# A retention-then-MLP kernel on one core: attention of the third group of units joins the stretches, with new values for load order and layouts

## The chip, the core and the metric

The kernel runs on one core of a Trainium2 chip. Times are device microseconds of one execution, from start to end on that core. The time before is a median of three runs. Engines are named as in the profile: PE is TensorE (matmuls), PEld its weight loads, DVE is VectorE, ACT is ScalarE, POOL is GpSimd (here it issues the loads), SP is SyncE (stores, and transposing transfers).

## What is computed

A retention layer (attention with a decay in place of the softmax) and, on its output, an MLP with an exact GELU:

```python
B, H, S, D = 8, 8, 576, 64                       # q, k, v
scores = matmul(q, k^T) / sqrt(D)
gamma  = 1 - 2 ** (-5 - h)                       # one for each head
Dmat   = where(i >= j, gamma ** (i - j), 0)
ret    = matmul(scores * Dmat, v)                # [B, H, S, D]
x      = ret -> [B * S, H * D]                   # 4608 tokens x 512
h      = x @ w_in                                # 512 -> 2048
g      = 0.5 * h * (1 + erf(h / sqrt(2)))
out    = g @ w_out                               # 2048 -> 512
```

Inputs and output are float32; the products run in bfloat16, with sums in float32.

## The kernel before

**Units and groups.** A sequence of 576 rows is cut into five chunks of 128 rows, the last with 64. A unit is one chunk of one batch entry, for all eight heads; the two short last chunks of two batch entries share one unit. There are 36 units, and they are put in groups of two (the short one is a group of its own): group 0 is units 0 and 1, group 1 units 2 and 3, group 2, the third, units 4 and 5, and so on. Four units make one block of 512 tokens, the `xT` tile; there are nine blocks. Units 4 to 7 make the second block.

**Attention of a unit.** Q and K are transposed (units 0 to 9 on TensorE, `turn`, which writes `qk_ps`; later ones by a transposing transfer from SP). Then come `scores` (`sc`), a multiplication with the decay mask on VectorE (`ret`), the products with V inside the chunk (`inner`, into `o_ps`), the running sum of K times V over the chunks (`state`, into `u_ps`, copied to `u_sb`), and the products of Q with that sum (`cross`, into `o_ps` too). V is scaled by the decay first (`scaled_v`, L826 on VectorE as one product for all heads, L829 on ScalarE as eight activations of 64 columns); the list `VH_ACT` says which units' V goes to ScalarE. The result is copied into `xT` on the way out of the accumulators.

**MLP of a block.** The first GEMM gives `hT` or, from the third block on, in parts, the accumulators `yT`, `zT` and `xT_` of seven products in place of eight (Strassen's scheme on 2 x 2 parts: "units" of the layout, with sums of weights `wi_sum` and of tokens `xs`). `LAYOUTS` says for blocks 2 to 8 in which order the four quarters of the first GEMM run: '0' is quarter 0 by seven products, '01' two quarters interleaved, 'p3' quarter 3 plain, '3p2' a quarter by seven interleaved with a plain one. The second GEMM (`oT`) is plain in the first block and by seven products in the others (`w_sum`, `s`). In the first block the first GEMM can start on a part of the tokens: a pair of column blocks runs as four pieces of 128 tokens each (`CUTS`), as units become ready, unless it stands in the list `WIDE`; then it runs at the full 512 tokens, when all four units are there.

**What sets the order.** The order of all engines is fixed when the program is built. A planner (`Plan`) keeps a clock for each engine, gives every operation a duration, a due time and the operations that it needs, and at each step issues what can start first. MLP products come from `stream`; `LOOK` says how far ahead in it the planner may pick. From a certain group on, the attention on TensorE is not planned product by product but as a list (`macro_of`): `inner` of both units of the group, the states behind it, scores of the next group where it is not in `APART`, and `cross`, issued one behind the other by `run_all`, due at the group's need plus `SHIFT`. In this document such a list is a stretch. Scores of a group in `APART` are a list of their own, due `BEFORE` ahead. `EARLY` says for which groups the lists are made: with 3, from the fourth group on; the operations of the first three are planned one by one.

```python
for n in range(EARLY + 1, len(groups) + 1):
    macros += [(n, names, need[n - 1] + SHIFT[n]) for names in macro_of(n)]
    if n in APART:
        macros.append((n, scores_of(groups[n]), need[n] - BEFORE))
```

**Loads.** All but the first unit's Q, K and V come through one queue that POOL issues, in the order of `ORDER`: `k2` is K of unit 2, `wi0` one eighth of `w_in`, `wo0` of `w_out`, `pos` a small table made on POOL in between. Units from 11 on follow in order of number. At most eight transfers are in flight. A unit's Q, K or V arrives as 128 KB, a weight piece as 256 KB.

**Filler.** While the planner's TensorE clock is under 16 us, `warm` fills each planned gap with products of zeros, of 512 columns, or 128 for the rest of a gap; eight of 512 stand at the very start.

All matmuls are issued by the helper `product` (L231) and the transposes by `turned` (L235), so the profile's rows are told apart by tiles.

Of the kernel before, what the change touches and what calls it, by code (L numbers as in the profile page):

```python
# [107 lines left out]
def kernel(  # L108
# [52 lines left out]
    def slot_of(i):  # L161
# [9 lines left out]
    N_VH = 5  # L171
    N_RET = 3
    N_Q = 4
    VH_ACT = [5, 6, 7, 8, 9, 10, 21, 22, 23, 24, 26, 27, 28, 29, 30, 31, 33, 34, 35]
    HOT = 10.1
    N_WARM = 8
    SLACK = 0.2
    CUTS = (0, 128, 256, 384, 512)
    AHEAD = 6
    WIDE = [2, 10, 14, 12, 4]  # L180
    VH_DUE = 14.0
    PARTS = 4
    FAST = 1
# [1 line left out]
    BUSY_FETCH = 6.2  # L185
    GAP_A = 4.7
    GAP_B = 0
    SHIFT = {4: -0.5, 5: 4.0, 6: 4.5, 7: -2.0, 8: 6.0, 9: 0.5, 10: 0.5, 11: -6.0, 12: -3.5, 13: -0.5, 14: -3.5, 15: -0.5, 16: -4.5, 17: -2.0, 18: -3.5, 19: 0.0, 20: 1.0}
    APART = [3, 5, 6, 7]
    BEFORE = 8.1  # L190
    UNIT_FROM = 2
    LOOK = 12
    HOLD = 6
    LAYOUTS = {2: ['01', '2', 'p3'], 3: ['01', '2', 'p3'], 4: ['1', '02', 'p3'], 5: ['0', '1', '2', 'p3'], 6: ['01', '23'], 7: ['01', '23'], 8: ['0', '12', 'p3']}
    LEAD = 8.9
    SPREAD = 5.6
    EASE = 9
    ORDER = ("k2 k1 pos q1 wi0 q3 k3 q2 v1 v2 v3 wi4 wi7 wi1 wi5 v4 k4 q5 wi6 k5 wi3 wi2 q4 wo0 v5 wo4 wo1 q9 wo5 "
             "q8 v7 wo6 v6 q7 q6 wo2 k7 v10 wo7 wo3 k6 q10 k8 v8 k10 k9 v9").split()
    K_ORDER = [0, 1, 8, 9, 2, 3, 10, 11, 4, 5, 12, 13, 6, 7, 14, 15]  # L200
    PRODUCTS = "3251467"
    SECOND = "1267534"
# [1 line left out]
    for t in range(UNIT_FROM, N_BLK):  # L204
        LAYOUT[t] = LAYOUTS[t]

# [99 lines left out]
    for t in range(N_BLK):  # L306
        if t < 2:
            cuts = CUTS if t == 0 else (0, 256, 512)
            for lo, hi in zip(cuts, cuts[1:]):
                stream.append([("1", t, m, 2, lo, hi) for m in K_ORDER[::2] if t or m not in WIDE])  # L310
            if t == 0:
                stream.append([("1", t, m + n, 1, 0, TOK) for m in WIDE for n in range(2)])
        else:
# [44 lines left out]
    pos = const.tile([128, 1, NCI], FP32, name="pos")  # L358
# [121 lines left out]
    def tiles_of(i):  # L480

        if i not in loaded:
            n = slot_of(i)
            if i in kept:
                loaded[i] = (const.tile([128, 2, H, D], BF16, name=f"qk_ld{i}"), const.tile([128, H, D], BF16, name=f"v_ld{i}"))
                return loaded[i]
            if n not in slots:
                ld_ring.take()
                slots[n] = (ld_pool.tile([128, 2, H, 2, D], BF16, tag="qk", name="qk_ld"),
                            ld_pool.tile([128, 2, H, D], BF16, tag="v", name="v_ld"))  # L490
            qk, v_ld = slots[n]
            j = units[i][2] or 0
            if i in old:
                loaded[i] = (qk.rearrange("p a (j h) b d -> p j a (h b) d", j=2)[:, j], v_ld[:, j])
            else:
                loaded[i] = (qk[:, :, :, j], v_ld[:, j])
        return loaded[i]
# [42 lines left out]
    for i in range(11, N_U):  # L540
        ORDER += [f"{what}{i}" for what in "qkv"]
    prev = ["val"]
    for item in ORDER:
        what = item.rstrip("0123456789")
# [325 lines left out]
    for n in reversed(range(len(groups) - 1)):  # L870
        need[n] = min(need[n], need[n + 1] - SPREAD)
    tiles_of(0)
# [2 lines left out]
            lambda engine, nm=nm: copy_on(engine, loaded[0][1] if nm == "v" else loaded[0][0][:, "qk".index(nm)], first[nm]),  # L875
            7.0 if nm == "v" else 5.2, at=lambda nm=nm: cast_at[nm])
    land = {}
    EARLY = 3
    ALONE = [groups[n][0] for n in range(2, len(groups)) if n in APART or groups[n - 1][0] not in fine]
    for i in range(N_U):  # L880
        bp, ci, j = units[i]
# [51 lines left out]
    for i in v_order:  # L933
# [3 lines left out]
        before = ["dv", f"land v{i}"] + ([f"vh{v_order[n - 1]}"] if n else [])  # L937
        if i in VH_ACT:
            step_ = H // PARTS
# [472 lines left out]
    def macro_of(n):  # L1412


        back, front = groups[n - 1], groups[n] if n < len(groups) and n not in APART else []
        states = states_behind(n - 1)
        if back[0] in fine:
            a = [f"in_a{back[0]}"] + [f"st_a{bp},{ci}" for bp, ci in states]
            b = [f"in_b{back[0]}"] + [f"st_b{bp},{ci}" for bp, ci in states]
            if front:  # L1420
                a, b = a + [f"odd_{front[0]}"], b + [f"even_{front[0]}"]
            return [a, b]
        ahead = scores_of(front)
        olds = [f"state{bp},{ci}" for bp, ci in states]
        if back[0] in tails:
            return [olds + [f"in_t{back[0]}"] + ahead]
        return [[f"inner{i}" for i in back] + olds + ahead + [f"cross{i}" for i in back if units[i][1]]]

    def scores_of(front):
        return [f"both_{i}" if i in fine or i in tails else f"scores{i}" for i in front if i not in fine or i == slot_of(i)]  # L1430

    def states_behind(n):

        if n < 0:
            return []
        i = groups[n][0]
        bp, ci, j = units[i]
        if j is None:
            return [(1, 0)] if bp == 0 else []
        return [] if (bp, ci) == (1, 0) else [(bp, ci)]  # L1440

    assigned = {}
    macros = []
# [4 lines that stand above are left out]
    in_macro = {nm for m in macros for nm in m[1]}  # L1448
# [98 lines left out]
    def pe_candidates():  # L1547
# [11 lines left out]
        for run in heads:  # L1559
# [4 lines left out]
            else:  # L1564
                look = run[:LOOK]
            for one in look:
# [23 lines left out]
    while True:  # L1590
        got = []
        for e in ("act", "dve", "pool", "sp"):
            b_ = P.best(e, SLACK if T[e] < 20.0 and e != "pool" else 0.05)
            if b_:
# [8 lines left out]
        if e == "pe":  # L1603
# [9 lines left out]
            else:  # L1613
                for run in heads:
                    got = [one for one in run[:LOOK] if f"mlp{one}" == op.name]
                    if got:
# [46 lines left out]
```

## Time and profile before

| | us |
|---|---|
| median of 3 runs | 280.59 (280.51 to 280.66) |
| the profiled execution | 281.12 |
| its span, first to last instruction | 279.2 |
| PE busy | 273.0 |
| DVE busy | 228.7 |
| ACT busy | 181.7 |
| POOL busy | 110.4 |
| last matmul starts | 275.7 |

The profiled execution's time holds 1.9 us around the span. A matmul's busy time in the rows is longer than the time to the next one's start, since they overlap; where the row says that 8 matmuls took so long, the next row's start tells how far apart they were issued. Rows of the timeline have start, duration, engine, line, operation and tiles, the number merged, and in brackets the idle time before and what ended it ("issue" where nothing that the profile shows ended it).

### The profile page before, as it was taken

Reading aid. Unit: us, or ns where it says so; the run is one execution under the profiler, and the core shown is the slowest. Engines: PE = TensorE matmul, PEld = TensorE weight load, DVE = VectorE, ACT = ScalarE, POOL = GpSimd, SP = SyncE. Lnnn points to the kernel's source line nnn. Section 1 sums busy time; section 2 is a strip of 40 time slices with the busy share of each in tenths; the row PEclk is TensorE's granted clock in tenths of the full one; section 3 lists DMA queues with packets and bytes.
Section 4 is the critical chain, followed back from the end, with each engine's and each line's share of the span. In section 5 each row is a group of like instructions: output and inputs, shape, how many; then the busy total and the mean of one; then the engine's idle time right before and its main releaser. Section 6 shows DMA issues by size and latency. Waiting matters only on the chain.

```text
span 279.2 us, 8727 instructions
## 1 busy us (share of the span) xinstructions
PE 273.0 (98%) x3626; PEld 216.2 (77%) x3626; DVE 228.7 (82%) x437; ACT 181.7 (65%) x446; POOL 110.4 (40%) x139
## 2 busy tenths in 40 slices
PE   7999999999999999999999999999999999999995
PEld 2675567478888688868886888778888888888684
DVE  5862554589989997999898999997899979969843
ACT  7766638786418823693559657975896689627840
POOL 8977688809755097311452725705000000000000
PEclk9999999999999999999999999999999999999999
DMA  9999999999999999999999999999600040003013
GB/s 150 161 187 179 190 175 173 178 169 165 149 142 177 193 134 151 134 236 99 142 197 88 128 160 222 116 113 121 190 2 2 6 151 2 2 22 131 0 40 113
DMA packets 152374, 35.55 MB, mean 127 GB/s; under 512 B 141072, under 2 KB 148240, under 8 KB 152336
## 3 DMA queue, kind: packets, MB, share of 16 engines
q0 software_dynamic: 115792, 17.97, 97.6%
q1 hardware_dynamic: 34544, 15.93, 31.0%
q10 hardware_dynamic: 2000, 1.11, 1.4%
q8 instruction: 28, 0.46, 0.7%
q14 instruction: 10, 0.08, 0.1%
HBM read 36.70 MB, written 9.44 MB: 165 GB/s over the span
## 4 chain that ended last, share of the span: by engine, by line
PE 79%; DMA 14%; POOL 5%; issue 1%; ACT 0%; DVE 0%; POOLq 0%
PE oT L231 37%; PE zT L231 11%; PE hT L231 9%; DMA w_out<-in_moe_w_out_dram 9%; PE yT L231 7%; PE o_ps L231 4%; DMA w_in<-in_moe_w_in_dram 3%; PE sc L231 2%; POOL qk_ld L522 2%; DMA qk_ld<-in_k_dram 2%; PE u_ps L231 2%; POOL w_in L528 1%; POOL v_ld L522 1%; PE xT__1851 L231 0%; PE xT__5150 L231 0%
## 5 line engine op out<-in xcount | busy, mean ns | idle before, releaser
L231 PEld LDWEIGHTS <-g 128*128 128x128 bf16 x576 | 55.2, 98 | 12.5 <-issue 0.4
L231 PEld LDWEIGHTS <-w_in 128*128 128x128 bf16 x528 | 47.2, 98 | 15.9
L231 PEld LDWEIGHTS <-wi_sum 128*128 128x128 bf16 x460 | 44.6, 98 | 7.1 <-issue 0.4
L231 PE MATMUL hT<-xT,w_in 128*128 128x256 bf16 (+2 forms) x344 | 49.0, 295 | 0.0
L231 PE MATMUL oT<-w_out,g 128*128 128x256 bf16 (+1 forms) x320 | 45.6, 294 | 0.1
L522 POOL DMA_DIRECT2D qk_ld<-in_q_dram x31 | 27.8, 898 | 38.9 <-DMA qkT<-qk_ld 24.2
L829 ACT ACTIVATE vh<-v_ld,dv 128x64 bf16<-128x64 bf16 x152 | 41.3, 348 | 1.0 <-DVE ret L657 1.0
L231 PEld LDWEIGHTS <-s 128*128 128x128 bf16 x384 | 36.8, 98 | 5.3 <-issue 0.4
L1104 ACT ACTIVATE g<-hT 128x512 bf16<-128x512 f32 (+1 forms) x58 | 31.5, 558 | 11.1 <-PE hT L231 10.4
L522 POOL DMA_DIRECT2D v_ld<-in_v_dram x31 | 28.0, 906 | 14.0 <-issue 6.7
L231 PE MATMUL oT<-w_sum,s 128*128 128x256 bf16 x256 | 32.6, 273 | 0.3 <-issue 0.3
L231 PE MATMUL oT<-w_sum,g 128*128 128x256 bf16 x256 | 31.1, 273 | 0.0
L1248 ACT COPY o_sb<-oT 128x512 f32<-128x512 f32 (+1 forms) x27 | 14.3, 539 | 23.7 <-PE oT L231 12.1
L522 POOL DMA_DIRECT2D qk_ld<-in_k_dram x31 | 28.0, 905 | 2.8 <-DMA v_ld<-in_v_dram 1.4
L1217 ACT ACTIVATE g<-zT 128x512 bf16<-128x512 f32 x46 | 26.4, 608 | 0.7 <-DVE zT L1226 0.6
L657 DVE TENSOR_TENSOR ret<-sc,msk 128x512 bf16<-128x512 f32 x36 | 22.9, 683 | 4.3 <-PE sc L231 4.3
L1252 DVE TENSOR_TENSOR o_sb<-o_sb,oT 128x512 f32<-128x512 f32 (+1 forms) x27 | 16.6, 626 | 10.5 <-PE oT L231 5.7
L834 ACT CAST u_sb<-u_ps 128x512 bf16<-128x512 f32 x19 | 11.3, 596 | 14.4 <-PE u_ps L231 12.5
L860 DVE TENSOR_TENSOR xT<-o_ps,dqT 128x512 bf16<-128x512 f32 x26 | 17.1, 683 | 1.9 <-PE o_ps L231 1.9
L573 DVE COPY qkT<-qk_ps 128x512 bf16<-128x512 bf16 x16 | 6.4, 421 | 13.9 <-PE qk_ps L235 13.8
L1226 DVE TENSOR_TENSOR zT<-q,zT 128x512 f32<-128x512 f32 x23 | 15.8, 692 | 2.1 <-PE zT L231 1.8
L575 ACT COPY q<-yT 128x512 f32<-128x512 f32 x16 | 9.0, 600 | 11.7 <-PE yT L231 11.7
(173 smaller groups left out, 470.6 us busy)
## 6 DMA issues: line engine op xcount, KB each, us to landing
out_dram<-o_sb SPq DMA_DIRECT2D x29, 256.0 KB, 3.4
qk_ld<-in_k_dram POOLq DMA_DIRECT2D x31, 128.0 KB, 7.2
qk_ld<-in_q_dram POOLq DMA_DIRECT2D x31, 128.0 KB, 7.5
v_ld<-in_v_dram POOLq DMA_DIRECT2D x31, 128.0 KB, 7.8
w_in<-in_moe_w_in_dram POOLq DMA_DIRECT2D x8, 256.0 KB, 8.1
w_out<-in_moe_w_out_dram POOLq DMA_DIRECT2D x8, 256.0 KB, 8.4
out_dram<-o_sb SPq DMA_DIRECT2D x7, 128.0 KB, 2.4
out_dram<-o_sb ACTq DMA_DIRECT2D x5, 128.0 KB, 1.9
```

The lines of the kernel that those rows point to most:

```text
L231: return nc.tensor.matmul(*args, **more)
L522: nc.gpsimd.dma_start(dst, src[2 * bp + j, :, ci * C:ci * C + C, :].rearrange("h s d -> s h d"))
L575: nc.scalar.copy(dst, src)
L657: nc.vector.tensor_tensor(r, t, by, op=ALU.mult)
L829: nc.scalar.activation(vh[:, h], loaded[i][1][:, h], AF.Copy, scale=dv[:, h, ci:ci + 1])
L834: ins = (nc.vector.tensor_copy if engine == "dve" else nc.scalar.copy)(u_sb[t if bp >= FINE else ci % 2], u_bank[1])
L860: nc.vector.tensor_tensor(dst, o, dqT[:, :, ci * C:ci * C + C], op=ALU.mult)
L1104: nc.scalar.activation(g_of(t, m0)[:, m0 % 2:m0 % 2 + n, m0 // 8, lo:hi], hT, AF.Gelu)
L1217: nc.scalar.activation(target(key, what), chain[key][n][1], AF.Gelu)
L1226: nc.vector.tensor_tensor(to, chain[key]["q"], z, op=ALU.add)
L1248: nc.scalar.copy(target(key, what), chain[key][n][1])
L1252: nc.vector.tensor_tensor(to, to, chain[key][n][1], op=ALU.add)
```

## The change

The values below are changed; no function is. `EARLY` goes from 3 to 2, which makes the list for the third group too (`SHIFT` gets an entry 3 for it). `WIDE` gets two more entries, so that of the first block's eight pairs one instead of three still runs in four pieces. `VH_ACT` goes from 19 units to 13: 5 to 9, 21, 23, 30, 31 and 34 go to VectorE, and 13, 15, 16 and 32 come to ScalarE. `APART` gets group 8. In `LAYOUTS` blocks 3, 5 and 8 change. `ORDER` is new, as are the shifts and the planner's `SLACK`, `BEFORE`, `LOOK` and `SPREAD`.

```diff
-    VH_ACT = [5, 6, 7, 8, 9, 10, 21, 22, 23, 24, 26, 27, 28, 29, 30, 31, 33, 34, 35]
+    VH_ACT = [10, 13, 15, 16, 22, 24, 26, 27, 28, 29, 32, 33, 35]
-    SLACK = 0.2
+    SLACK = 0.4
-    WIDE = [2, 10, 14, 12, 4]
+    WIDE = [14, 2, 10, 0, 4, 12, 8]
-    SHIFT = {4: -0.5, 5: 4.0, 6: 4.5, 7: -2.0, 8: 6.0, 9: 0.5, 10: 0.5, 11: -6.0, 12: -3.5, 13: -0.5, 14: -3.5, 15: -0.5, 16: -4.5, 17: -2.0, 18: -3.5, 19: 0.0, 20: 1.0}
-    APART = [3, 5, 6, 7]
-    BEFORE = 8.1
+    SHIFT = {3: 2.0, 4: 0.0, 5: -7.0, 6: -3.0, 7: -4.5, 8: 0.5, 9: -2.0, 10: -2.5, 11: -0.5, 12: 0.5, 13: -6.0, 14: -0.5, 15: -2.0, 16: 1.0, 17: -4.0, 18: 1.5, 19: 1.5, 20: 6.5}
+    APART = [3, 5, 6, 7, 8]
+    BEFORE = 7.2
-    LOOK = 12
+    LOOK = 18
-    LAYOUTS = {2: ['01', '2', 'p3'], 3: ['01', '2', 'p3'], 4: ['1', '02', 'p3'], 5: ['0', '1', '2', 'p3'], 6: ['01', '23'], 7: ['01', '23'], 8: ['0', '12', 'p3']}
+    LAYOUTS = {2: ['01', '2', 'p3'], 3: ['3', '20', 'p1'], 4: ['1', '02', 'p3'], 5: ['01', '3p2'], 6: ['01', '23'], 7: ['01', '23'], 8: ['3', '20', 'p1']}
-    SPREAD = 5.6
+    SPREAD = 6.5
-    ORDER = ("k2 k1 pos q1 wi0 q3 k3 q2 v1 v2 v3 wi4 wi7 wi1 wi5 v4 k4 q5 wi6 k5 wi3 wi2 q4 wo0 v5 wo4 wo1 q9 wo5 "
-             "q8 v7 wo6 v6 q7 q6 wo2 k7 v10 wo7 wo3 k6 q10 k8 v8 k10 k9 v9").split()
+    ORDER = ("k3 k1 wi0 q2 q3 q1 k2 wi3 v2 v3 pos wi4 v1 wi7 wi1 v4 wi5 wi2 k4 q5 q4 k5 wo0 wi6 q8 v5 wo4 q9 wo5 "
+             "wo1 q6 v6 v7 k10 k7 wo7 wo2 v10 wo6 wo3 k6 q7 q10 k8 k9 v9 v8").split()
-    EARLY = 3
+    EARLY = 2
```

## The prediction

> **What bounds the kernel now.** I read the engine totals first, then TensorE's waits, then its rows in order of time, then the load queue.
>
> ```profile
> PE 273.0 (98%) x3626; PEld 216.2 (77%) x3626; DVE 228.7 (82%) x437; ACT 181.7 (65%) x446; POOL 110.4 (40%) x139
> ...
> PEclk9999999999999999999999999999999999999999
> DMA  9999999999999999999999999999600040003013
> ...
> q8 instruction: 28, 0.46, 0.7%
> ```
>
> TensorE is busy for 98% of the span at full granted clock. The DMA engines are over 90% busy for the first 29 of 40 slices, which is some 200 us.
>
> ```profile
> PE warm L231 <- DVE ln_scale L352: 1.2, 1, 1.2
> PE qk_ps L235 <- DMA qk_ld<-in_k_dram: 0.7, 1, 0.7
> PE oT L231 <- issue: 0.3, 1, 0.3
> PE zT L231 <- ACT g L1217: 0.2, 1, 0.2
> ```
>
> Those are all its waits (engine, line, releaser, total, times, longest). So the end is set by how much TensorE has to issue, plus a few waits under 1 us. A matmul's cost is the distance between starts, since neighbours overlap.
>
> ```profile
> 15.49 0.81 PE L231 MATMUL warm<-u_sb 128*128 128x512 bf16 x3
> 16.23 0.74 PE L231 MATMUL o_ps<-ret,v_ld 128*64 128x128 bf16 x16
> 16.90 0.62 PE L231 MATMUL hT<-xT,w_in 128*128 128x128 bf16 x8
> 17.45 0.44 PE L231 MATMUL u_ps<-vh,qk_ld 128*64 128x64 bf16 x16
> 17.82 8.45 PE L231 MATMUL hT<-xT,w_in 128*128 128x128 bf16 x68
> 26.11 0.61 PE L235 MATMUL qk_ps<-ident,qk_ld 128*128 128x128 bf16 x8
> ...
> 51.35 1.90 PE L231 MATMUL oT<-w_out,g 128*128 128x512 bf16 x8
> 53.92 0.61 PE L235 MATMUL qk_ps<-ident,qk_ld 128*128 128x128 bf16 x8 [0.68 <-DMA qk_ld<-in_k_dram]
> ...
> 149.89 2.59 PE hT L231 x12
> 263.75 12.24 PE oT L231 x112
> ```
>
> The last two rows are of the chain of waits: 12 matmuls of 512 columns in 2.59 us make 0.216 us each, 112 of 256 columns in 12.24 us make 0.109. The 68 from 17.82 to 26.11 are 40 of 128 columns and 28 of 512, so one of 128 takes (8.29 - 28 x 0.216)/40 = 0.056. Before 17.45 TensorE waits for loads and masks and passes the time in filler (warm); from 17.45 it is never idle by more than a few tenths, except at 53.92. There it stands 0.84 us (start 53.92, less the 0.22 us of the matmul before it, which starts at 52.87) for the K rows of units 8 and 9, the last load that TensorE itself transposes. The load queue is thus a second bound, up to 53.92.
>
> **The change, part by part.** Counts are of the two programs' instructions, engine by engine.
>
> *Third group in a stretch* (EARLY 2). For units 4 and 5 before had state and inner products in one interruption of the MLP (0.92 us between the MLP matmuls around 35.0) and cross products in another (0.44 us at 36.3). After has all three in one, as the stretch from 80.54 to 81.81 has: 1.26 us. 1.36 - 1.26 = 0.10 us saved. It hides nothing else; scores still stand apart.
>
> *WIDE, 5 entries to 7.* 64 matmuls of 128 columns become 16 of 512: 16 x 0.216 - 64 x 0.056 = -0.1 us. All other working matmuls stay in number and shape, so the layouts and shifts move work and cost TensorE nothing by themselves.
>
> *Start.* Filler grows from 17 to 24 of 512 columns and falls from 13 to 10 of 128. At 0.22 to 0.44 us for the first kind (warm rows from 9.56 on) and 0.06 to 0.2 for the second, that is 1.0 to 2.9 us more. The reason is the load order: v1 goes from the eighth load to the twelfth, behind wi0, wi3 and wi4. In the landing records of the trace the first load lands at 7.42 and the last K at 53.79, with 25 unit loads, 16 weights and three tail pairs in this stretch. 0.88 us a unit load, 1.33 a weight and 1.0 a tail pair give those ends and, within 0.8 us, every landing between. So v1 lands at about 7.42 + 8 x 0.88 + 3 x 1.33 = 18.4 (13.75 before). Its scaled values take 0.68 us of VectorE (the vh row's mean), behind masks and two decay rows; the state product, at 17.45 before, comes at 19.1 to 19.7. With equal work done ahead of it this is 1.65 to 2.25 us late. I take 1.9.
>
> *The load queue up to the last K.* One load (v8) that stood ahead of k9 now stands behind it; everything else ahead of it is the same set. The last K's transposes can thus start at 53.92 - 0.88 = 53.04, not earlier. From the state product to them after has 32.7 us of TensorE work (56 matmuls of 512 columns and 8 of 128 for the first block, 48 of the second GEMM, 48 of 256, 40 transposes, attention by the rows above), so TensorE would be there at 51.8 to 52.4 and waits 0.7 to 1.3 us, some of it already at the K rows of 6 and 7 and at q7, which land at 49.2 and 50.1 and are wanted at 48.7 and 49.6 or half a microsecond later. The late start is swallowed by this wait: up to here the queue is the bound, not the sum.
>
> *What is left behind the last K.* After has done less by then: four matmuls of 512 columns of the second GEMM (0.86), eight of 256 columns of the first (0.87) and one set of scores (0.67, the row at 77.25) stand behind it that stood before it. That is 2.40 us more to do from 53.04 than before had from 53.92.
>
> *Waits further on.* Before has two past 54 us, of 0.43 and 0.38:
>
> ```profile
> 108.44 0.28 PE L231 MATMUL oT<-w_sum,s 128*128 128x256 bf16 x1
> 108.98 0.92 PE L231 MATMUL oT<-w_sum,s 128*128 128x256 bf16 x7 [0.26 <-issue]
> ...
> 171.04 0.60 PE L231 MATMUL xT__3421<-xs,wi_sum 128*128 128x256 bf16 x4
> 171.85 0.60 PE L231 MATMUL zT<-xs,wi_sum 128*128 128x256 bf16 x4 [0.21 <-ACT g L1217]
> ```
>
> The first has no releaser. It falls inside a run of equal matmuls, at TensorE's 1371st. The instruction queue brought 28 transfers of 16 KB for 7,252 TensorE instructions, about 128 matmuls each, and one was in flight from 106.4 to 107.6. I read it as an instruction block coming late: these 128 matmuls hold two stretches and took 5.9 us, while the other blocks up to 187 us took 6.6 us or more and show no such wait. (Later ones take 4.4 to 4.9 us without one, the first of them while no load was in flight, from 187.8 to 189.9.) After's shortest block up to 200 us has 6.7 us of work, so I take the 0.43 off. [...]
>
> The second is in block 5, whose three units ran one after another, in '0', '1', '2'; after pairs 0 with 1, and I take 0.38 off. Against it I put 0.3 for one new wait of this size somewhere in a new order (bounds: 0, and 0.84, the largest wait here).
>
> *Scaled V.* ScalarE loses 48 activations of 64 columns (152 to 104, 0.27 us busy each), VectorE gains six products and, with copies, nine instructions: 6 x 0.68 + 2 x 0.42 + 0.69 = 5.6 us on 228.7. Units 5 to 9 move to VectorE between 20 and 60 us, where it works 19.9 of 40 us; 13, 15 and 16 move away from it between 60 and 100, where it works 39.0 of 40. It costs nothing as long as that slack holds; without it, up to one product (0.68).
>
> Sum past the last K: -0.88 + 2.40 - 0.43 - 0.38 + 0.3 = +1.0 us (the two savings of 0.10 lie ahead of the last K, inside the wait). The profiled execution took 281.12 us with a span of 279.2, so 282.1 for it; its 0.53 us above the median of 280.59 belongs to that execution, so 281.6 for the median.
>
> **Rivals.**
>
> *The start decides, no change.* If the loads run 0.9 us quicker up to the last K (2% of 46 us), TensorE never waits there, and the end is the start's delay plus a sum without waits. For: k9's neighbours k8 and v8 landed 0.5 to 0.6 us later than the rates say, beside the first block's stores (issued at 51.12), which come about 1 us later in after. Against: k9 itself is on the rate. Start +1.9, savings -0.2, waits -0.30 (32.70), -0.84, -0.43, -0.38: -0.25, so 280.3; with a start at 19.7 and the new wait, 281.0.
>
> *Faster: the load queue keeps the pace of its best stretch.* From wo1's landing at 34.41 to wo7's at 46.36, seven unit loads, four weights and a tail pair took 11.95 us, where the rates make it 12.5: 4% less. If all of after's loads ran so, the last K's transposes could start at 53.04 - 0.04 x 46.4 = 51.2 and v1 would land 0.5 us sooner, so that TensorE is there at 51.3 and nothing waits: 51.3 - 53.92 + 2.40 - 0.43 - 0.38 = -1.0, so 279.6. It decides from a last K's transpose before 51.8. For: that stretch has no stores of the first block beside it, and after's stores come later. Against: its gain was gone again at k6 (49.10, on the rates), two loads after wo7.
>
> *VectorE becomes the bound between 60 and 210 us.* It gains units 21, 23, 30, 31, 34 there and loses 13, 15, 16, 32: one net product. If two masks or sums come one product late each: +1.4 on the forecast, 283.0. For: 39.0 of 40 us. Against: TensorE shows one wait of 0.2 us on a chain with ScalarE, none on VectorE.
>
> *The stretch isn't formed.* After's program has the units' inner, state and cross products in one run, so this is out; it would cost the 0.10 us.
>
> **How the numbers follow.** Forecast (queue-bound to the last K, then 2.4 us more work) 0.54, the start deciding 0.22, faster 0.16, VectorE 0.08. The unknown ends: the last K's transposes from 52.2 (the start decides below it) to 53.6 (late by the 0.6 of its neighbours), waits from none to both old ones and 0.84. Low: 281.6 - 0.8 - 0.3 = 280.5, taken down to 280.1 into the second case; high: 281.6 + 0.6 + 0.8 = 283.0. Below 280.1 lies most of the faster case and little else. A measurement of this kernel tells 0.2%, 0.56 us, from no change: faster is under 280.0, slower over 281.15. The faster case and the lower edge of the second give 0.18; the middle of the second and the lower end of the first 0.24; the rest 0.58.
>
> **What would show it.** State product of units 0 and 1 at 19.1 to 19.7; a TensorE wait on a K load at about 53 us, with shorter ones at 48 to 51; from that transpose to the last matmul 223.5 to 224.3 us (221.9 before); no wait without releaser near 100 us; units 4 and 5 in one interruption of about 1.26 us. The forecast is wrong if the last K's transposes start before 52.2, or if waits past 54 us come to over 2 us.

## The result, and the profile after

The changed kernel takes 281.63 us (median of 5 runs, 281.59 to 281.98); the kernel before, on the same chip, 280.66 (280.51 to 281.29). The ratio is 1.0032, with a 95% interval of 1.0018 to 1.0046: slower by about 1 us. On another chip, 12 runs of the changed kernel against 34 of the old one gave 281.98 and 280.65, a ratio of 1.004 (1.0024 to 1.0057). The profiled execution took 281.63, its span 279.5.

The page of the changed kernel, engine totals and shares of the chain that ended last:

```profile
PE 273.8 (98%) x3582; PEld 215.3 (77%) x3582; DVE 232.5 (83%) x446; ACT 168.9 (60%) x391; POOL 110.3 (39%) x139
...
PE 97%; ACT 1%; DVE 1%; issue 0%; DVEq 0%
```

VectorE is busy 3.8 us longer and ScalarE 12.8 us less, as the diff of `VH_ACT` says. The chain that ended last, which was 79% TensorE and 14% DMA before, is now TensorE almost alone: in this execution no load stands in it. TensorE's waits, all of them (line, releaser, total, times, longest):

```profile
PE warm L231 <- DVE ln_scale L352: 1.2, 1, 1.2
PE hT L231 <- ACT xT L575: 0.6, 2, 0.5
```

The K wait, the unreleased wait and the one on `g` of before are gone; two at the start have come. TensorE's timeline of the changed kernel (start, duration, line, tiles, number):

```profile
14.95 1.95 PE L231 MATMUL warm<-u_sb 128*128 128x512 bf16 x9
16.83 0.64 PE L231 MATMUL o_ps<-ret,v_ld 128*64 128x128 bf16 x16
17.92 1.09 PE L231 MATMUL hT<-xT,w_in 128*128 128x128 bf16 x16 [0.46 <-ACT xT L575]
18.95 0.41 PE L231 MATMUL o_ps<-ret,v_ld 128*64 128x128 bf16 x8
19.19 0.67 PE L231 MATMUL u_ps<-vh,qk_ld 128*64 128x64 bf16 x16
...
37.27 0.64 PE L231 MATMUL o_ps<-ret,vh 128*64 128x128 bf16 x16
37.74 0.42 PE L231 MATMUL u_ps<-vh,qk_ld 128*64 128x64 bf16 x16
38.09 0.42 PE L231 MATMUL o_ps<-qkT,u_sb 64*64 64x128 bf16 x16
...
50.62 1.89 PE L231 MATMUL oT<-w_out,g 128*128 128x512 bf16 x8
52.42 0.61 PE L235 MATMUL qk_ps<-ident,qk_ld 128*128 128x128 bf16 x8
...
88.41 0.60 PE L231 MATMUL yT<-xs,w_in 128*128 128x256 bf16 x4
89.08 1.09 PE L231 MATMUL zT<-xs,wi_sum 128*128 128x256 bf16 x8
...
274.33 1.91 PE L231 MATMUL oT<-w_sum,g 128*128 128x256 bf16 x16
```

The reader sees: the first state product at 19.19 (17.45 before). Units 4 and 5 in one interruption, inner, state and cross products one behind the other. The transposes of the last K at 52.42 without a bracket: eight matmuls of 0.216 us from 50.62 are issued by 52.35, and K of unit 9 had landed at 52.29 by the landing records, so TensorE and the load arrive together. And one new wait: 0.67 us lie between the start of four matmuls at 88.41 and the next row; they take 0.44, so TensorE waits 0.24 us, from about 88.84.

One measure carries the rest: the distance from the start of the last K's first transpose to the start of the last matmul, "the tail" from here on. It was 275.70 - 53.92 = 221.78 us before and is 275.97 - 52.42 = 223.55 after.

### The profile page after: what moved, and what is told of

Its sections match the earlier page's. It is cut to its first block, busy times and chain, and to the rows that moved or that the text cites. A ratio compares the mean times of both kernels' runs of the same rounds, so it can differ in the third digit from the quotient of the medians.

```text
span 279.5 us, 8588 instructions
## 1 busy us (share of the span) xinstructions
PE 273.8 (98%) x3582; PEld 215.3 (77%) x3582; DVE 232.5 (83%) x446; ACT 168.9 (60%) x391; POOL 110.3 (39%) x139
## 4 chain that ended last, share of the span: by engine, by line
PE 97%; ACT 1%; DVE 1%; issue 0%; DVEq 0%
PE oT L231 41%; PE hT L231 16%; PE zT L231 11%; PE yT L231 7%; PE o_ps L231 5%; PE warm L231 4%; PE sc L231 3%; PE qk_ps L235 2%; PE u_ps L231 2%; ACT xT L575 0%; ACT g L1217 0%; PE xT__3495 L231 0%; PE xT__2739 L231 0%; PE xT__4682 L231 0%; PE xT__4055 L231 0%
## 5 line engine op out<-in xcount | busy, mean ns | idle before, releaser
L231 PEld LDWEIGHTS <-w_in 128*128 128x128 bf16 x480 | 45.3, 98 | 18.3 <-issue 0.6
L231 PE MATMUL hT<-xT,w_in 128*128 128x512 bf16 (+2 forms) x296 | 49.6, 316 | 0.6 <-ACT xT L575 0.6
L231 PE MATMUL oT<-w_sum,s 128*128 128x256 bf16 x256 | 31.9, 273 | 0.0
L829 ACT ACTIVATE vh<-v_ld,dv 128x64 bf16<-128x64 bf16 x104 | 28.8, 347 | 0.0
L575 ACT COPY q<-yT 128x512 f32<-128x512 f32 x19 | 10.7, 595 | 19.9 <-PE yT L231 19.9
L573 DVE COPY qkT<-qk_ps 128x512 bf16<-128x512 bf16 x18 | 7.2, 421 | 12.7 <-PE qk_ps L235 12.7
L826 DVE TENSOR_TENSOR vh<-v_ld,dv 128x512 bf16<-128x512 bf16 x23 | 15.7, 685 | 1.3 <-DMA v_ld<-in_v_dram 1.3
```

The source lines that it names most:

```text
L231: return nc.tensor.matmul(*args, **more)
L575: nc.scalar.copy(dst, src)
L826: nc.vector.tensor_tensor(vh, loaded[i][1], dv[:, :, ci:ci + 1].to_broadcast([128, H, D]), op=ALU.mult)
L829: nc.scalar.activation(vh[:, h], loaded[i][1][:, h], AF.Copy, scale=dv[:, h, ci:ci + 1])
```

## Experiments

Each is timed in the same rounds as the kernel before, whose median was 281.04 in the first four, 280.73 in the next four and 280.65 in the last four.

**1. The kernel before once more, unchanged.**

> The kernel before, unchanged, profiled once more. Open is whether its three TensorE waits past 50 us (0.84 us on a K load at 53, 0.43 with no releaser at 108, 0.38 at 171) come back. Theory 'the profile is typical': all three return within 0.1 us, and the profiled execution again takes the median plus a few tenths. Rival 'the waits belong to one execution': one or two are absent or below half, and the profiled time falls to about 280.5; then 0.5 us of what the change seemed to save in the traces was never in the median.

Measured: 280.88 us, ratio 0.9995 (0.9978 to 1.0011). Its profiled execution took 280.60. Timeline of TensorE in it:

```profile
53.65 0.61 PE L235 MATMUL qk_ps<-ident,qk_ld 128*128 128x128 bf16 x8 [0.46 <-DMA qk_ld<-in_k_dram]
...
108.17 1.05 PE L231 MATMUL oT<-w_sum,s 128*128 128x256 bf16 x8
109.06 1.04 PE L231 MATMUL oT<-w_out,s 128*128 128x256 bf16 x8
```

The unreleased wait at 108 isn't there: eight matmuls stand together where the execution shown before the prediction had one, a gap and seven. The K wait is 0.62 us in place of 0.84 (K of unit 9 landed at 53.52). The wait at 171 is there again (0.38 us by the distance between starts), and the tail is 275.02 - 53.65 = 221.37. So the wait at 108 belongs to single executions, the K wait and the one at 171 to the kernel; of the two expectations the rival was nearer.

**2. K of units 8 and 9 issued earlier.** Before, with six slots of the load order exchanged; only POOL's order changes.

```diff
+    INSTEAD = {"q10": "k8", "k8": "v8", "v8": "k9", "k10": "v9", "k9": "q10", "v9": "k10"}
```

> The kernel before, with its order on every engine but one row of loads: k8, v8, k9, v9 are issued before q10 and k10. By the rate of 0.88 us a load, k9 lands at about 51.9 in place of 53.8. Theory 'the load queue holds TensorE at 53 us': the 0.84 us wait goes, all behind it comes 0.8 us earlier, span 278.4, time 0.5 to 0.8 us below before. Rival 'the load is not what counts': the wait is taken over by a later load (the transposes of unit 10, whose loads come 3 us later) or by the scaled V of unit 8, and the time stays within 0.3 us.

Measured: 280.32, ratio 0.9977 (0.9963 to 0.999). The last K's transposes start at 53.13 with no wait. The time falls by about as much as that wait was (281.04 - 280.32 = 0.72 us; the wait was 0.84 and 0.62 in two executions), so in the old kernel the load queue did set the end up to here. And the wait near 108 is back, larger, with no releaser:

```profile
107.65 0.28 PE L231 MATMUL oT<-w_sum,s 128*128 128x256 bf16 x1
108.72 0.93 PE L231 MATMUL oT<-w_sum,s 128*128 128x256 bf16 x7 [0.78 <-issue]
```

1.07 us between starts, less 0.11 for one matmul: 0.96 us. The tail is 222.31, that is 221.36 and this wait.

**3. and 4. The same, with the instruction stream moved.** 72 and 103 matmuls more, of the same total of columns: fillers of 512 columns are cut in four of 128, and products of the first block in two or four. The borders of the blocks of about 128 matmuls (3,626 over 28 transfers of the instruction queue make 129.5) thus fall on other work.

```diff
+    IN_TWO, IN_FOUR, FILLERS = 9, 0, 12     (72 more)
+    IN_TWO, IN_FOUR, FILLERS = 7, 3, 13     (103 more)
```

> As the run with k9 early, and 12 filler products and 36 real ones of 512 columns at the start are cut into pieces, 72 more matmuls for about 0.1 us. It moves the borders of TensorE's instruction blocks by 72 matmuls, so that the shortest block up to 187 us has 6.96 us of work. Theory 'the 0.43 us at 108 us is a late instruction block': it is gone and none appears elsewhere; span some 0.4 us below the run with k9 early alone. Rival 'something else holds that matmul': the wait stays at the same place in the program, 8 matmuls into the second GEMM's run, and nothing is gained.

> The same with 103 more matmuls in place of 72, which puts a block border so that one block, from the scores at 51 us on, has 5.2 us of work, and one at 189 us 5.8. Theory 'late instruction block' (5.94 us of work and 0.43 of waiting make 6.4 us the least that a block takes while loads run): the wait at 108 us is gone, and one of about 1.2 us with no releaser stands near 57 us, one matmul group past the stretch there, perhaps a smaller one near 131. Rival 'something else': 0.43 us at the old place and nothing near 57.

Measured with 72: 280.62, ratio 0.9983 (0.9968 to 0.9998). No unreleased wait of that size; tail 274.76 - 53.38 = 221.38. But the state product comes at 17.95, 0.3 to 0.5 us late:

```profile
16.43 0.74 PE L231 MATMUL o_ps<-ret,v_ld 128*64 128x128 bf16 x16
17.40 0.62 PE L1125 MATMUL hT<-xT,w_in 128*128 128x128 bf16 x8 [0.23 <-DMA w_in<-in_moe_w_in_dram]
17.95 0.44 PE L231 MATMUL u_ps<-vh,qk_ld 128*64 128x64 bf16 x16
```

The cut filler did not take the time: behind it the inner products start at 16.43, as in run 2 (16.44). TensorE then waits for a piece of `w_in`, 0.39 us by the distance between starts (0.63 with 103), which landed at 17.35 (17.48 with 103) and at 16.35 in run 2. The first transfer of the instruction queue began at 14.61 here and at 14.82 with 103, against 17.16 in run 2; whether it delayed that load was not tried. With 103: 281.91, ratio 1.0034 (1.002 to 1.0048). No wait at 108, and two elsewhere:

```profile
130.43 0.41 PE L231 MATMUL sc<-qkT 64*64 64x128 bf16 x13
131.50 0.47 PE L231 MATMUL sc<-qkT 64*64 64x128 bf16 x19 [0.66 <-issue]
...
187.75 0.19 PE L231 MATMUL sc<-qkT 64*64 64x64 bf16 x1
188.71 0.19 PE L231 MATMUL sc<-qkT 64*64 64x64 bf16 x1 [0.77 <-issue]
```

Both cut a run of equal products, the first 32 scores into 13 and 19. By the program's count they are at matmuls 1754 and 2520 of TensorE (the profile lacks 13 records); 766 = 6 x 127.7 lie between. The wait of run 2 was at the 1371st, and 383 = 3 x 127.7 lie from there to the first. So the waits sit on a fixed grid of some 128 matmuls that stays while the work is moved over it. What fell is my rule for which border waits: the block with 5.2 us of work, less than the 5.9 at 108, had none near 57 us, where a wait was expected; near 131, where only a smaller one was put down as possible, there was one of 0.85 us.

**5. A late start in the old kernel.** Eight more fillers of 512 columns behind the ninth.

```diff
+        if len(fillers) == LATE:
+            for _ in range(8):
+                nc.tensor.matmul(t, lhsT=zeros[:, :128], rhs=zeros, start=True, stop=True)
```

> The kernel before, with eight more filler products of 512 columns ahead of the inner products of units 2 and 3: TensorE's start is 8 x 0.216 = 1.73 us later, everything else in place. Theory 'a late start is swallowed by the wait on the last K': of the 1.73 us the 0.6 to 0.8 us of that wait take up their part, the wait is gone or under 0.1, and the time rises by 0.9 to 1.1 us. Rival 'the queue moves along with TensorE' (loads later too): the wait stays and the time rises by 1.7. Rival 'the start has slack': under 0.3 us.

Measured: 282.59, ratio 1.0075 (1.0048 to 1.0102), with few runs and a wide spread (281.73 to 284.4). In the profile the state product comes at 19.07, 1.6 us late; the last K's transposes at 54.41 (53.92 and 53.65 in the two of before) and unwaited. Against the profile predicted from, two waits for loads that are gone, 0.30 at 32.7 and 0.84 at the last K, take up 1.14 of the 1.62 us, so a late start in the old kernel is in part swallowed, as forecast. The time rose by 1.86, not by the 0.9 to 1.1 expected. A border near 109 is part of that:

```profile
108.59 0.34 PE L231 MATMUL o_ps<-qkT,u_sb 64*64 64x128 bf16 x7
109.77 0.30 PE L231 MATMUL o_ps<-qkT,u_sb 64*64 64x128 bf16 x7 [0.84 <-issue]
```

1.02 us here, eight products earlier in the program than before, as eight fillers stand ahead: the border keeps its number, not its work. The tail is 222.45, and the last matmul comes 1.16 us later than in the profile predicted from, of which 0.59 is the larger border wait (1.02 against 0.43).

**6. The changed kernel with `EARLY = 3`,** the third group in single products again, planned anew.

> The changed kernel with EARLY back at 3 alone, planned anew: the third group's state and inner products stand apart from its cross products again; filler, loads and the start stay as in the changed kernel. Theory 'the stretch is worth its 0.10 us and no more': within 0.3 us of the changed kernel, start and last K as there. Rival 'the stretch is what moves the time' (either way): 0.6 us or more apart.

Measured: 282.28, ratio 1.0062 (1.0043 to 1.008). The changed kernel itself was not in these rounds; in later ones on the same chip it was 281.98, with an interval that overlaps (1.0024 to 1.0057). In the profiles the last matmul starts at 276.53, against 275.97 and 276.31 in two of the changed kernel. The stretch is thus worth a few tenths at most, and not told from nothing.

**7. The kernel before with the load order of after,** planned anew with its own layouts and shifts (`ORDER` alone changed).

> The kernel before with the changed kernel's load order alone, planned anew. Theory 'the load order makes the late start': the state product comes 2 us or more later than at 17.45 (40 pieces of 128 columns ahead of it where before has 24, so the start counts from 0.9 us sooner), no wait on the last K, the 0.38 us at 171 stays; 0.6 to 1.3 us above before. Rival 'the cut of the first GEMM (WIDE) makes it': the start at most 0.5 us later, the time no higher than before.

Measured: 284.84, ratio 1.0145 (1.0125 to 1.0165). The state product comes at 21.20 (a set of 16 more products of the first GEMM runs ahead of it), and the K wait is gone. New ones come:

```profile
80.10 0.30 PE L231 MATMUL o_ps<-ret,vh 128*64 128x128 bf16 x4 [0.21 <-DVE ret L657]
80.70 0.30 PE L231 MATMUL o_ps<-ret,vh 128*64 128x128 bf16 x4 [0.30 <-DVE ret L657]
81.30 0.30 PE L231 MATMUL o_ps<-ret,vh 128*64 128x128 bf16 x4 [0.29 <-DVE ret L657]
```

The expectation (0.6 to 1.3 us above before, the wait at 171 as it was) missed: the time rose by 4.1 us, and no wait stands at 171. Masks on VectorE come too late here for one unit, the thing that the rival on VectorE had feared for the changed kernel. The order alone makes the late start, and it needs the other values of the change beside it: with all of them the same order costs 1 us, not 4. The three waits are 1.3 us by the distances between starts, of the 4.9 by which the tail, 226.26, is longer than 221.37; the rest was not taken apart.

**8. Run 2 with 72 more matmuls, all of them in products of the first block.** No filler is cut.

```diff
+    IN_TWO, IN_FOUR, FILLERS = 6, 4, 0
```

> The run with k9 early and 72 more matmuls, but with all cuts in the real products of 512 columns behind the start (4 sets of four in four, 6 in two), none in the filler. Theory 'cut filler cost the 0.5 us at the start there': state product back at 17.5 to 17.7, no wait at 108 us, 0.3 us for the cuts, span about 278.1, and 0.8 to 1.2 us below before. Rival 'the cuts in the filler cost nothing, the chip or the loads did': the state product at 17.9 again and the time as in the first such run.

Measured: 280.22, ratio 0.9979 (0.9968 to 0.9991), level with run 2 by the ratio; its last matmul, at 274.50, is the earliest of all profiles. The state product is at 17.47 (the piece of `w_in` landed at 16.34, the instruction transfer began at 17.00), the tail 221.36, and only the wait of block 5 is left:

```profile
169.84 0.60 PE L231 MATMUL xT__3493<-xs,wi_sum 128*128 128x256 bf16 x4
170.65 0.60 PE L231 MATMUL zT<-xs,wi_sum 128*128 128x256 bf16 x4 [0.21 <-ACT g L1245]
```

**9. The changed kernel once more, unchanged.**

> The changed kernel once more, unchanged, beside the three runs below. Theory (the start and the load queue meet at the last K; waits at the borders of 128 matmuls come and go with the execution): first state product at 19.1 to 19.3, last K's transposes at 52.4 to 52.7, from there to the last matmul 223.5 to 224.0 us plus whatever border waits this execution has (0 to 1.0), ratio to before 1.001 to 1.005. Rival (the wait-free trace of after is the rule for it): no wait above 0.25 us past 20 us at all, and the last matmul within 0.1 us of 275.97.

Measured: 281.98, ratio 1.004 (1.0024 to 1.0057). State product at 19.61, last K landed at 52.52 and transposed from 52.77 without a wait, the 0.24 again at 89.1, tail 276.31 - 52.77 = 223.54. The state product missed its range (19.1 to 19.3) by 0.3. The wait for the copy of `xT` ahead of it is no reason, since it is as long in the first profile of after (0.46 in brackets in both); the 0.42 us by which all is later stand already in the filler that starts at 11.53 here and at 11.11 there. No border wait came, though there was room for one in the theory.

**10. v1 four places earlier in the changed kernel.** Planned anew; 22 fillers of 512 columns in place of 24, all else ahead of the tail the same in kinds and numbers.

```diff
-    ORDER = ("k3 k1 wi0 q2 q3 q1 k2 wi3 v2 v3 pos wi4 v1 wi7 ...
+    ORDER = ("k3 k1 wi0 q2 q3 q1 k2 wi3 v1 v2 v3 pos wi4 wi7 ...
```

> The changed kernel with v1's load four places earlier (right behind wi3), orders planned again; all work past the first state product keeps its kinds and numbers, two fillers of 512 columns and one of 128 fall away ahead of it. Theory (v1's place makes the start late, and start and queue meet at the last K): first state product at 18.2 to 18.8 instead of 19.19; the 0.4 to 1.0 us won there come back as TensorE waits at the K and Q loads of units 6 to 9, so the last K's transposes still start at 52.3 to 52.6 and the last matmul is within 0.2 us of the changed kernel's. Rival 1 (the start alone decides): the last matmul comes earlier by the whole 0.4 to 1.0 us and no wait on a load appears. Rival 2 (v1 is not what holds the start): first state product at 19.0 or later.

Measured: 281.86, ratio 1.0035 (1.0018 to 1.0051): no gain. Timeline of TensorE:

```profile
18.98 0.44 PE L231 MATMUL u_ps<-vh,qk_ld 128*64 128x64 bf16 x16
...
34.98 0.62 PE L235 MATMUL qk_ps<-ident,qk_ld 128*128 128x128 bf16 x8 [0.18 <-DMA qk_ld<-in_q_dram]
...
52.72 0.61 PE L235 MATMUL qk_ps<-ident,qk_ld 128*128 128x128 bf16 x8 [0.22 <-DMA qk_ld<-in_k_dram]
```

The start is 0.63 us earlier than in run 9 and 0.21 earlier than in the first profile of after, less than the theory's 18.2 to 18.8 and just short of rival 2's 19.0, although v1 landed at 14.87 in place of 17.63. What the start won stands in two waits for loads, 0.35 and 0.38 by the distances between starts, and the last K's transposes and the last matmul (276.27) are within 0.05 us of run 9's. The start alone does not decide.

**11. The same, and k8 and k9 ahead of q10.**

```diff
+    INSTEAD = {"q10": "k8", "k8": "k9", "k9": "q10"}
```

> The same, and k8 and k9 are issued ahead of q10 (a tail pair, 0.7 to 1.0 us of queue); TensorE's order is that of the run before it. Theory (start and queue meet): with both sides moved the last K lands at about 51.4 and its transposes start at 51.7 to 52.1; q7 (landed at 49.83 in the changed kernel, wanted there at 50.2) now bounds the gain, so the last matmul comes 0.2 to 0.6 us earlier than in the run before it. Rival (the load queue is no bound in the changed kernel): no difference to the run before it, within 0.1 us.

Measured: 281.37, ratio 1.0019 (1.0004 to 1.0033).

```profile
34.72 0.62 PE L235 MATMUL qk_ps<-ident,qk_ld 128*128 128x128 bf16 x8
...
52.15 0.61 PE L235 MATMUL qk_ps<-ident,qk_ld 128*128 128x128 bf16 x8
```

The time is 0.49 us below that of run 10, in the same rounds. The start is that of run 10 (18.96), the transposes come 0.57 us earlier and unwaited, the tail is 223.56, and the last matmul starts 0.56 us earlier. So in the changed kernel the start and the load queue meet at the last K: the start alone gained nothing, both together did. The loads alone were not tried; run 9, where TensorE came to the last K without a wait, leaves them nothing to gain. (It was not q7 that bounded the gain, as expected, but the Q load at 34.7, where 0.12 us is still waited.)

**12. Run 8 with block 5 in after's layout,** planned anew from there.

```diff
-    LAYOUTS = { ... 5: ['0', '1', '2', 'p3'], ...
+    LAYOUTS = { ... 5: ['01', '3p2'], ...
```

> Before with the K rows of units 8 and 9 issued earlier, 72 of its MLP matmuls cut in parts, and block 5's units paired as 01, 3p2, planned again from block 5 on. Theory (the 0.38 us wait at 171 is made by block 5's layout): it is gone, no other of that size takes its place at 160 to 180 us, the last matmul comes at about 274.1 (274.50 with the old layout) and the time is 279.7 to 280.1, ratio to before 0.994 to 0.998. Rival (any layout has such a wait somewhere in the block, as after's 0.24 at 88.7): a wait of 0.2 to 0.5 us stands elsewhere past 150 us and the last matmul is within 0.15 us of 274.50.

Measured: 280.76, ratio 1.0001 (0.9984 to 1.0018), so worse than run 8 (single times 280.60 to 281.96 here, 279.97 to 280.67 there, on the same chip). The wait at 171 is gone, and three others have come:

```profile
179.28 1.03 PE L1125 MATMUL hT<-xT,w_in 128*128 128x512 bf16 x4
180.45 0.60 PE L231 MATMUL xT__3662<-xs,wi_sum 128*128 128x256 bf16 x4
...
190.46 0.60 PE L231 MATMUL oT<-w_out,s 128*128 128x256 bf16 x4
191.23 1.03 PE L231 MATMUL oT<-w_sum,s 128*128 128x256 bf16 x8 [0.17 <-ACT o_sb L1276]
...
208.06 0.60 PE L231 MATMUL zT<-xs,wi_sum 128*128 128x256 bf16 x4
208.80 0.60 PE L231 MATMUL xT__4228<-xs,wi_sum 128*128 128x256 bf16 x4
```

By the distances between starts 0.31, 0.33 and 0.31 us; the tail is 275.18 - 53.23 = 221.95, longer by 0.59 (0.95 less 0.38 is 0.57). The rival was nearer, though it had the last matmul within 0.15 us of 274.50 and it came at 275.18: the layout moves such a wait, and what comes in its place is made by the whole plan behind it.

## Why the prediction held, and where its steps were off

The prediction, 281.6 us, and its direction held. Its reasons did in the main. Two of its terms were mis-sized, and it was luck that they cancelled; the wait that it put at the last K did not come; and one thing said of the median was not so. The tails tell it:

| kernel, one profiled execution each | last K transposed | last matmul | tail | waits at borders in it |
|---|---|---|---|---|
| before, as predicted from | 53.92 | 275.70 | 221.78 | 0.43 |
| before again (1) | 53.65 | 275.02 | 221.37 | none |
| k8, k9 early (2) | 53.13 | 275.44 | 222.31 | 0.96 |
| 72 more (3), (8) | 53.38, 53.14 | 274.76, 274.50 | 221.38, 221.36 | none |
| 103 more (4) | 53.58 | 276.81 | 223.23 | 0.85, 0.93 |
| late start (5) | 54.41 | 276.86 | 222.45 | 1.02 |
| after | 52.42 | 275.97 | 223.55 | none |
| after again (9) | 52.77 | 276.31 | 223.54 | none |
| v1 early (10), and k8, k9 (11) | 52.72, 52.15 | 276.27, 275.71 | 223.55, 223.56 | none |

Where no border wait stands, the tail is 221.36 to 221.38 in the old kernel and 223.54 to 223.56 in the new one; with their waits taken off, the others come to 221.35 to 221.45. Runs 6, 7 and 12, whose plans differ behind the last K too, have tails of their own: 223.75, 226.26 and 221.95.

*What is left behind the last K, +2.40 us: right.* The tails differ by 2.18; the old one's wait of 0.38 gone and the new one of 0.24 leave 2.18 + 0.38 - 0.24 = 2.32 of work, against 2.40 counted. With the last matmul's own 0.11 after's tail is 223.66, in the range named (223.5 to 224.3).

*The new wait, +0.3 us somewhere: right in size,* 0.24 at 88.7 in all four profiles in the table's last three lines.

*Block 5's wait, -0.38: right for this plan.* It is gone after; run 12 shows that this is no property of the layout alone.

*The last K's turn, -0.88 us (transposes at 53.04, reached at 51.8 to 52.4, after a wait of 0.7 to 1.3): the size was off.* They started at 52.42, 1.50 earlier than in the profile predicted from, and at 52.77 in the second profile; the means of two each are 53.79 and 52.60, so -1.19. The wait of 0.7 to 1.3 us there, with shorter ones at 48 to 51, was a sign that the prediction named, and neither profile has it: TensorE was there at 52.35, as forecast, and in run 9 at 52.77, and the last K had landed 0.06 and 0.25 us before. The step that failed is the queue's pace. By the landing records k6 came at 48.81 (49.2 by the rates) and q7 at 49.83 (50.1), so the queue had gained 0.3 to 0.4 us by then and more behind; in run 9 they came at 49.02 and 50.07 and k9 at 52.52, nearer to the rates. This is in part the mechanism that the rival "the start decides" named (loads 0.9 us quicker), without its price, since the work left behind is the same either way. Why the queue ran quicker was not tried.

*The late start, +1.9 us, "swallowed by this wait": half right.* State product at 19.19 and 19.61 (19.1 to 19.7 named), but the reason named, v1's landing, has a small part at most, and that the value held is in part luck: v1 landed at 17.63 and 17.69, not 18.4, and with v1 2.8 us earlier still (runs 10 and 11) the state product comes at 18.98 and 18.96, 0.2 us before that of the first profile. In all five profiles of kernels with the changed values TensorE waits ahead of it for the copy of `xT` (the row at 17.92), 0.62 us by the distance between starts; what sets the moment of that copy was not tried. And nothing is swallowed in the changed kernel, which has no wait there; start and queue are equal bounds, as runs 10 and 11 show: the start alone gains 0.04 us on run 9, both 0.60 (276.31 to 275.71).

*The late block, -0.43: the wrong kind of number.* The cause is borne out by the grid that keeps its numbers (runs 2, 4 and 5) and by the landings at the end of this document; the rule taken from it, by the length of a block, is not (run 4). The page of before has 28 transfers of 16 KB on the instruction queue for TensorE's 7,252 instructions, 259 to a transfer or some 130 matmuls with their weight loads, beside the grid's measured step of 127.7 matmuls; all borders in these profiles were crossed without such a wait but those with the five waits of 0.43 to 1.02 us in the table. But it is a wait of single executions, 0 and 0.43 us at one border of one program (0.96 with two loads moved), and so no fixed term of a sum. Taking it off the profiled execution was right, off the median it was not.

*"Its 0.53 us above the median of 280.59 belongs to that execution":* so it did, but against run 1, whose profiled execution took 280.60, its last matmul is 0.68 later, and 0.43 of that is the border and 0.22 the longer K wait, which the sum had also counted as gains. Between typical executions the account is -1.19 + 2.18 = +1.0 us; between the two profiled ones it is -1.50 + 2.40 - 0.43 - 0.38 + 0.24 = +0.33, and the last matmul came 0.27 later. The medians rose by 0.97 and 1.33. The prediction got +1.0 by taking 0.3 too little off at the last K and 0.43 too much at the border.

*VectorE's 5.6 us hidden: right.* Its busy time grew by 3.8, and no wait past 20 us names it. *The stretch:* 1.26 us in one piece, as counted (37.18 to 38.44); its 0.10 cannot be told.

Seen from the start the same account reads: from the state product to the last matmul the changed kernel takes 256.78 and 256.70 us, the old one 258.25 and 257.45. The new order is shorter by 0.7 to 1.5 us there and begins 1.7 to 2.0 us later. The old kernel with k8 and k9 early and its stream moved (run 8) begins at 17.47 and needs 257.03, and beats both.

## What to carry to other kernels

Where TensorE is busy all the time and one load is waited for on the way, count the work left behind that load: its difference between two plans came out to a tenth, while landing times and waits were off by 0.3 to 0.8 us. Before a wait is taken off in a sum, look whether it is there in a second execution (the one at 108 us was 0.43 in one and none in the next); and when two bounds meet, an edit that moves one of them can show nothing (0.04 us in run 10, 0.60 with both moved in run 11), so move both before calling either harmless.

## What the hardware showed

Waits without a releaser, 0.43 to 1.02 us, stand on a grid of some 128 matmuls (127.7 between the waits of runs 2 and 4), in some executions of one kernel and not in others (0.43 in before, none in run 1). The instruction queue's records go with it. At the border near 108 us, the transfer of 16 KB ahead of it began at 106.37, 106.14 and 106.88 us in the three executions that waited (before, runs 2 and 5), with 60 to 75 matmuls left to the border, and landed 1.3 to 1.6 us before TensorE went on. In run 1, with no wait, it began at 103.97, with 89 matmuls left, and landed 3.4 us before the border. The two waits with 103 more matmuls ended 1.3 and 1.4 us after a landing too. Counting the other borders in steps of 127.7 matmuls from there, in all fourteen profiles, every border crossed without such a wait came 1.5 us or more after its 16 KB had landed. So by these records the wait is for a transfer that lands late; what delays its start is open. Moving the grid by 72 matmuls took the wait away in both runs that had it so, moving it by 103 made two; the length of the blocks did not tell which borders would wait.
